# Batch 1 of a sliding-window attention and MoE kernel: q, k and attention output turned by DMA instead of on TensorE, with a new order

## The chip, the core and the metric

The kernel runs on one core of a Trainium2 chip. The metric is the device time of one execution in microseconds (us), taken as the median of several runs of the same kernel. PE is TensorE, DVE is VectorE, ACT is ScalarE, POOL is GpSimd and SP is SyncE, which in this kernel only issues DMA transfers.

## What is computed

There are 4 batches of 768 tokens with 8 heads of 64 elements. Each query sees the first 4 keys (the sinks) and its own window of 128 keys. The attention output of the 3072 tokens, 512 wide, then goes through a two-layer network with a squared ReLU.

```python
# attention, per batch and head: q, k, v are (768, 64)
scores = q @ k.T / 8
keep = (key position < 4) | (0 <= query position - key position < 128)
a = softmax(where(keep, scores, -1e9))
x = concat over heads of (a @ v)          # (3072, 512), tokens of all batches
h = x @ w_in                              # w_in is (512, 2048)
out = (maximum(h, 0) ** 2) @ w_out        # w_out is (2048, 512)
```

## The kernel before

A batch is 6 tiles of 128 tokens, and most work goes by stages s = 0, 1, 2 of 256 tokens (two tiles). Everything is computed in bf16 with fp32 accumulation in PSUM.

Scores need q and k with the head dimension on partitions, but they are loaded with tokens on partitions. So each tile of q and k has to be turned, 128x128 at a time. Batch 0's first four tiles are loaded by SP, regrouped to bf16 and turned on PE. For tiles 4 and 5 of batch 0 and all of batch 1, POOL issues loads that cast to bf16 on the way (`load_cast`, L507, into the tile `qn`). The function `transpose` (L637) then turns them on PE into PSUM (`pt`), and `unload` copies them to `qkT` on DVE or ACT. Batch 1 is turned in two groups: tokens 0 to 511 are group 0 and tokens 512 to 767 are group 1. For batches 2 and 3 (`NATURAL`), the loads are the same kind (`load_natural`, L535), but SP issues a DMA that turns one tile of q or k, 128 tokens by 512, straight into `qkT` (L591).

For each stage, `scores` (L744) writes the products to PSUM, ACT takes the exponential (L764), DVE (L776) or POOL (L355) masks it, and `values` (L812) multiplies it with v. The sinks have their own small product for the whole group (`sink_scores`, L703, with the keys that `sink_keys`, L679, copies out of `qkT` to `kblk`). `norm` (L828, L829) divides and writes `xn_sb`, again with tokens on partitions.

The network's first layer needs these rows turned as well. For batches 0 and 1, `bridge` (L861) turns the eight 128x128 blocks of a stage on PE into `px`, in two halves, and `bridge_copy` copies them to `xT`. For batches 2 and 3, `turn_x` (L843) issues two DMAs per stage on SP that write `xT`. The name `TURNED` lists stages of batch 1 that go this way; it is empty before.

`layer1` (L890) multiplies with `w_in`, for stages 0 and 1 together in columns of 512 tokens, and for stage 2 alone in columns of 256. Batch 0 does stages 0 and 1 apart. ReLU (L901 on ACT, L903 on DVE) and squaring (L912 or L910) follow. The second layer is `layer2` (L931) for the first two stages of batch 0. It is `layer2_fast` elsewhere (L1042), which makes seven products of quarter size where eight would be needed, with sums on DVE beforehand (L1000) and afterwards (L1067, L1083, L1090). Outputs are stored by SP (L954, L1115, and at the very end L1108, L1120, L1121).

The order on every engine is written by a planner (`Plan.run`) when the kernel is built. It takes the operations that are ready, places the one with the earliest planned start, and breaks ties by a key. Each operation has a planned cost; a DMA has in addition a planned time to landing, part of which is its `margin`. `PLACES` shifts and stretches the keys of whole groups of operations, and `NUDGES` shifts single ones, by their number. `LATENCY` is the planned time of a signal between engines. What comes out is a fixed sequence of instructions for each engine, each waiting only for its own inputs and buffers. While an early part runs, `warm` (L322) fills half of each planned idle stretch of PE before 34 us with products of the identity that nobody reads.

SP is one such sequence: a store that waits for its data holds back every turn behind it. DMAs of all queues share the same 16 DMA engines.

Of the kernel before, what the change touches and what calls it, by code (L numbers as in the profile page):

```python
# [16 lines left out]
LATENCY = 0.122  # L17
# [5 lines left out]
    ('att', 0, 0): (-2.46, 0.47, -0.66), ('att', 0, 1): (-0.14, 1.62, -0.14), ('att', 0, 2): (-1.375, 1.42, -0.64),  # L23
    ('att', 1, 0): (0.765, 0.89, 0), ('att', 1, 1): (-0.28, 2.29, -0.72), ('att', 1, 2): (0.08, 1.3, -0.06),
    ('att', 2, 0): (-0.07, 1.27, 0), ('att', 2, 1): (1.14, 0.56, -0.28), ('att', 2, 2): (-1.285, 1.05, -0.48),
    ('att', 3, 0): (0.09, 1.14, 0.06), ('att', 3, 1): (0.4, 1.06, -0.08), ('att', 3, 2): (-0.465, 1.16, -0.56),
    ('ev', 0, 2): (-0.46, 0.74, 0.02), ('ev', 1, 0): (-0.01, 0.91, -2.78), ('ev', 1, 1): (-0.165, 1.04, 0),
    ('ev', 1, 2): (-0.025, 0.87, 0.02), ('ev', 2, 0): (0.11, 0.96, 0), ('ev', 2, 1): (-0.045, 0.93, 0.36),
    ('ev', 2, 2): (-1.3, 0.62, 1.04), ('ev', 3, 0): (0.22, 2.01, -1.96), ('ev', 3, 1): (0, 1, -0.42),
    ('ev', 3, 2): (0.04, 1.07, -0.02), ('l1', 0, 0): (-0.28, 2.16, -0.32), ('l1', 0, 1): (-0.035, 0.33, -0.46),  # L30
    ('l1', 0, 2): (1.69, 0.27, -0.42), ('l1', 1, 0): (0.825, 0.61, -0.02), ('l1', 1, 2): (-0.155, 0.96, 0.14),
    ('l1', 2, 0): (0.035, 0.76, -0), ('l1', 2, 2): (-2.375, 1.53, -0.32), ('l1', 3, 0): (0.025, 1.07, -0.42),
    ('l2', 0, 0): (0.32, 2.21, -0.22), ('l2', 0, 1): (0.44, 1.69, 0.06), ('l2', 0, 2): (-4.315, 2.49, -0.54),
    ('l2', 1, 0): (0, 1.01, 0), ('l2', 1, 1): (2.345, 1.97, 0.22), ('l2', 1, 2): (-0.41, 0.56, 0.12),
    ('l2', 2, 0): (-0.41, 0.41, -0.6), ('l2', 2, 1): (-0.47, 0.26, 0.66), ('l2', 2, 2): (0, 1.01, 0),
    ('l2', 3, 0): (-0.09, 1.06, 0), ('l2', 3, 2): (-0.12, 0.72, 2.76), ('prep', 0, 0): (4.54, 2.5, -1),
    ('prep', 0, 1): (-1.04, 0.71, -0.64), ('prep', 1, 0): (0.935, 2.5, -0.44), ('prep', 3, 0): (-0.495, 2.45, 0.1),
    ('sink', 0, 0): (-0.755, 0.62, -0.54), ('sink', 0, 1): (0.135, 0.98, -0.04),
    ('sink', 1, 0): (-0.375, 1.71, 0.04), ('sink', 1, 1): (0.365, 0.61, 0.08), ('sink', 2, 0): (-0.01, 2.21, 0.06),
    ('sink', 3, 0): (-0.045, 0.9, 0), ('sum', 0, 2): (0, 1, -0.2), ('sum', 1, 0): (0.345, 0.25, -2.82),  # L40
    ('sum', 1, 1): (-0.27, 0.85, 0.08), ('sum', 1, 2): (-0.61, 0.73, -0.3), ('sum', 2, 0): (-0.06, 0.53, 1.32),
    ('sum', 2, 1): (-0.185, 1.13, 0.06), ('sum', 2, 2): (1.225, 2.25, -1.82), ('sum', 3, 0): (-0.005, 0.78, -0.5),
    ('sum', 3, 1): (-0.08, 0.34, 0.58), ('sum', 3, 2): (-0.185, 1.76, 0.42), ('turn', 0, 0): (4.705, 1.71, -0.76),
    ('turn', 0, 1): (0.09, 1.27, -0.04), ('turn', 0, 2): (1.185, 0.93, -0.3), ('turn', 1, 0): (0, 1.04, 0),
    ('turn', 1, 1): (0.995, 1.58, 0.4), ('turn', 1, 2): (0.65, 0.38, 0.02), ('turn', 2, 0): (0.67, 0.92, 0.14),
    ('turn', 2, 1): (-0.005, 0.93, -1.56), ('turn', 2, 2): (0.105, 1.4, 0.26), ('turn', 3, 0): (-0.1, 1.13, 0.08),
    ('turn', 3, 1): (-0.045, 0.55, -0.08), ('turn', 3, 2): (0.095, 1.46, -0.1),
    ('val', 0, 0): (-3.365, 0.71, -0.66), ('val', 0, 1): (0.145, 1.37, 0), ('val', 0, 2): (-1.82, 0.34, -3),
    ('val', 1, 0): (-0.355, 1.14, 0.04), ('val', 1, 1): (1.24, 2.09, -0.76), ('val', 1, 2): (0.18, 1.66, -2.5),
    ('val', 2, 0): (4.08, 1.76, -1.82), ('val', 2, 1): (0.05, 1.41, 0), ('val', 3, 0): (-1.585, 0.72, -0.38),  # L50
    ('val', 3, 1): (0.115, 0.58, -0.88), ('val', 3, 2): (-0.1, 1.09, -0.02), ('wt', 0): (0.275, 0.55, 0.32),
}
NUDGES = {
    4: (-0.366, 1.44), 16: (0, -0.3), 17: (0.072, -1.02), 18: (-0.061, -1.08), 19: (0.005, -0.02),
    20: (0.18, -0.98), 21: (0.025, -1.52), 24: (0, -0.44), 25: (-0.338, -1.38), 26: (0.71, 1.9),
    27: (-0.006, -0.32), 28: (0.484, 0.84), 29: (0, -0.36), 30: (-0.027, 0.14), 31: (0.007, -0.26), 32: (0, -0.48),
    33: (-0.136, -2.88), 34: (-0.096, 0.58), 35: (-0.031, 0.88), 36: (-0.018, 0), 37: (0.103, 0.12),
    39: (0.084, 0.7), 41: (-0.017, 0.88), 42: (0, -0.36), 43: (-0.11, 0.72), 44: (0, -0.12), 45: (0.297, 0.68),
    46: (-0.172, -1.86), 47: (-0.011, 0), 48: (-0.112, -0.02), 49: (-0.039, 1.08), 50: (-0.207, 0.22),
    51: (-0.044, 1.66), 52: (-0.002, -0.14), 53: (-0.017, -1.04), 54: (0, -0.2), 56: (-0.203, 0.34),  # L60
    58: (0.029, -0.48), 59: (0.008, 0), 60: (0.204, -1.22), 61: (0.19, 0.54), 62: (-0.101, -1.14), 63: (-0.022, 0),
    64: (0.192, 0.18), 65: (-0.153, 0.14), 66: (0.306, 0), 67: (0, -0.12), 69: (0.192, -2.78), 70: (-0.072, 0),
    71: (-0.012, 0), 72: (0, 0.38), 73: (-0.071, -0.04), 74: (-0.001, 0.16), 75: (-0.154, 0.08), 76: (0.133, -0.02),
    77: (0.57, 1.32), 78: (0.012, 0.46), 81: (-0.043, 0.3), 82: (0.016, -2.06), 83: (0.261, -0.22), 84: (-0.009, 0),
    86: (0.047, -0.02), 87: (0.257, -0.48), 88: (-0.361, 0.4), 89: (-0.047, 0.42), 90: (0.15, 0.34),
    91: (-0.217, 0), 92: (0, -0.06), 93: (0.05, -0), 94: (-0.016, 0), 95: (0.007, 0.02), 98: (0.071, -1.36),
    99: (-0.204, 0.84), 100: (0.062, -0.24), 101: (0, 0.08), 102: (0.126, 0.34), 103: (-0.194, -0.22),
    104: (0.051, 0), 105: (-0.214, -0.16), 108: (0.126, 0), 109: (0.206, 0), 110: (0.582, 0.28), 111: (0.032, 0.44),
    113: (-0.082, 0.1), 114: (-0.531, 0.32), 115: (0.058, -0.02), 116: (-0.003, -0.42), 118: (0.141, -1.44),
    119: (-0.307, 0.3), 120: (0.009, 0.06), 121: (0.002, 0), 122: (-0.044, 0.36), 123: (-0.017, 0.24),  # L70
    125: (-0.069, 0.34), 126: (0.099, -0.44), 127: (0, 0.14), 128: (-0.238, -0.62), 129: (-0.154, -0.08),
    130: (-0.003, 0), 131: (-0.296, 0.4), 132: (-0.082, -0.32), 133: (0.024, -0.38), 134: (0.073, 0),
    135: (0.059, 0.06), 136: (0.065, 0), 137: (0.021, 0.44), 138: (-0.166, 0.68), 139: (0.012, 0.3),
    140: (0.032, -0.28), 141: (-0.189, 0), 143: (0.103, 0), 144: (0.071, -0.44), 145: (-0.059, 0),
    146: (-0.436, 0.38), 148: (0.164, -0), 150: (0.527, -1.46), 151: (-0.19, 0.24), 153: (0.033, 0), 155: (0, 0.04),
    156: (0.089, 0), 157: (0.185, -0.32), 158: (-0.173, 0.56), 159: (-0.171, 0.18), 160: (0.252, 0.52),
    161: (-0.034, 1), 162: (-0.113, 1.42), 163: (0.013, 0.48), 165: (-0.127, 0.32), 166: (0.044, 0.4),
    167: (-0.035, 0.68), 169: (0, -0.14), 170: (-0.137, 0), 171: (-0.007, 0.26), 172: (0, 0.16),
    174: (-0.066, -0.92), 175: (0.19, 0.58), 177: (0.091, 0), 178: (0.319, -0.4), 179: (-0.18, 1.08),
    180: (-0.069, 0.02), 181: (-0.338, 0.2), 182: (-0.006, -0.02), 185: (-0.471, 1.5), 186: (-0.092, 0),  # L80
    187: (0.214, -0.08), 188: (0.107, -0.42), 189: (0.232, 0), 190: (0.088, 0), 192: (0, -0.16), 193: (-0.003, 0),
    194: (-0.01, -0.06), 196: (0.202, -0.16), 197: (0.001, -0.26), 198: (-0.511, 0), 199: (0.009, -1.34),
    200: (0.532, 0.1), 201: (-0.061, -1.16), 202: (-0.007, 0), 204: (-0.154, 0.18), 205: (0.379, 0.36),
    206: (-0.08, 0.86), 208: (0.012, -1.06), 209: (-0.163, -1.22), 210: (-0.013, 0), 211: (0.032, 0.04),
    212: (-0.121, 0), 213: (0, -0.2), 214: (0, 1.06), 215: (0, -0.06), 216: (0.121, 0.78), 217: (-0.108, 0),
    218: (0.25, 0.48), 219: (-0.155, 0), 220: (0.299, -0.24), 221: (0, -0.16), 222: (0, -0.3), 223: (-0.2, 0),
    224: (-0.065, 0), 225: (0, -0.38), 226: (0.019, -0.14), 228: (0.152, -0.9), 229: (-0.183, -0.86),
    230: (-0.164, 0), 231: (-0.021, 0.6), 232: (0.141, 0.18), 233: (-0.345, 0.26), 236: (0.132, -2.36),
    237: (0.017, -0.1), 238: (0, 0.72), 239: (-0.152, 0.14), 240: (-0.106, 0.48), 241: (-0.058, 0.3),
# [165 lines left out]
def kernel(  # L255
# [11 lines left out]
    nc = tc.nc  # L267
# [958 lines left out]
```

## Time and profile before

| | us |
|---|---|
| median of 3 runs | 216.98 |
| lowest and highest | 216.52 and 217.19 |
| the profiled execution's own time | 216.81 |
| its span, first to last instruction | 215.1 |

| engine | busy, us | share of the span |
|---|---|---|
| PE, matmul | 207.5 | 96% |
| DVE | 145.1 | 67% |
| ACT | 117.8 | 55% |
| POOL | 88.9 | 41% |

The granted TensorE clock is 1.0 throughout. The profiled execution is 0.17 us under the median, and 1.71 us of its time lie outside of the span. Matmuls are pipelined, and their shown durations overlap: the profile gives 309 ns as the mean of one L890 product, while 16 of them in a row take 1.75 us in the chain. So the pace of PE is read from the starts of successive blocks, not from the mean duration.

### The profile page before, as it was taken

What the parts mean: (1) busy time and instruction counts of PE and PEld (TensorE: products, weight loads), DVE (VectorE), ACT (ScalarE), POOL (GpSimd) and SP (SyncE); (2) the same over time, 40 slices, a digit from 0 to 9 for tenths busy, and PEclk for the clock granted to TensorE, in tenths of its full rate; (3) what the DMA queues carried; (4) which work ended last, traced back from release to release, by engine and by line L of the source; (5) the groups of instructions that cost most, each with busy time, mean ns of one, the idle gap of its engine ahead of it and who ended that gap; (6) DMA issues with size and microseconds to landing.
All of it is one profiled execution on the core that took longest, in us unless ns stands there. A gap on an engine that the chain in (4) does not pass through costs nothing.

```text
span 215.1 us, 5182 instructions
## 1 busy us (share of the span) xinstructions
PE 207.5 (96%) x2177; PEld 161.0 (75%) x2184; DVE 145.1 (67%) x276; ACT 117.8 (55%) x147; POOL 88.9 (41%) x127
## 2 busy tenths in 40 slices
PE   7999989999999999999999999999999999999992
PEld 7759977688667688554889765884988855799892
DVE  6488446687965767966788758779983543466652
ACT  3687857538954367688651627668411046657210
POOL 7999373698988963089405002227000000000000
PEclk9999999999999999999999999999999999999999
DMA  5999999999999999999959977010142220000222
GB/s 178 259 178 207 171 202 212 160 142 199 149 144 165 189 188 156 137 126 110 141 53 139 144 174 172 12 40 0 27 76 98 97 101 0 0 5 0 98 101 98
DMA packets 93351, 26.06 MB, mean 121 GB/s; under 512 B 86800, under 2 KB 91280, under 8 KB 93328
## 3 DMA queue, kind: packets, MB, share of 16 engines
q0 software_dynamic: 69248, 12.59, 77.9%
q1 hardware_dynamic: 23896, 13.07, 30.3%
q8 instruction: 17, 0.28, 0.6%
q10 hardware_dynamic: 184, 0.07, 0.1%
q14 instruction: 6, 0.05, 0.1%
HBM read 27.30 MB, written 6.29 MB: 156 GB/s over the span
## 4 chain that ended last, share of the span: by engine, by line
PE 81%; DMA 8%; DVE 4%; POOL 3%; issue 1%; ACT 1%; POOLq 0%
PE pm L890 35%; PE py L1042 28%; PE po L812 6%; PE py L931 6%; DMA qn<-in_q_dram 5%; PE ps L744 4%; DMA w_in_sb<-in_moe_w_in_dram 4%; POOL qn L507 1%; PE pt L637 1%; POOL v L516 1%; DVE qkT L331 1%; PE ya L1042 1%; POOL vs L685 1%; PE px L861 1%; DVE r L903 1%
## 5 line engine op out<-in xcount | busy, mean ns | idle before, releaser
L890 PE MATMUL pm<-xT,w_in_sb 128*128 128x256 bf16 (+1 forms) x576 | 88.3, 309 | 0.3 <-ACT r L901 0.2
L890 PEld LDWEIGHTS <-w_in_sb 128*128 128x128 bf16 x576 | 62.4, 114 | 20.9 <-issue 2.1
L901 ACT ACTIVATE r<-pm 128x1024 bf16<-128x1024 f32 x41 | 42.0, 1025 | 38.9 <-PE pm L890 37.4
L764 ACT ACTIVATE expm<-ps 128x1024 bf16<-128x1024 f32 (+1 forms) x48 | 43.5, 951 | 12.7 <-PE ps L744 12.5
L912 DVE TENSOR_TENSOR gT<-r 128x1024 bf16<-128x1024 bf16 x34 | 24.1, 712 | 21.0 <-ACT r L901 20.6
L355 POOL TENSOR_SCALAR_AFFINE_SELECT expm<-expm 128x512 bf16<-128x512 bf16 x26 | 18.2, 725 | 44.6 <-ACT expm L764 37.2
L1042 PEld LDWEIGHTS <-gT 128*128 128x128 bf16 x336 | 31.3, 98 | 3.7 <-issue 0.3
L1042 PEld LDWEIGHTS <-sg 128*128 128x128 bf16 x240 | 22.8, 98 | 3.9 <-issue 0.9
L1042 PE MATMUL py<-wt,sg 128*128 128x256 bf16 x160 | 20.8, 273 | 0.1
L1042 PE MATMUL py<-wt,gT 128*128 128x256 bf16 x160 | 20.7, 273 | 0.0
L1042 PE MATMUL py<-w_out_sb,gT 128*128 128x256 bf16 x144 | 18.7, 273 | 0.0
L812 PEld LDWEIGHTS <-expm 128*128 128x128 bf16 x352 | 16.3, 97 | 2.3 <-issue 0.9
L829 DVE TENSOR_TENSOR xn_sb<-po,rc 128x512 bf16<-128x512 f32 (+1 forms) x28 | 17.2, 615 | 1.0
L812 PE MATMUL po<-v,expm 128*128 128x65 bf16 x352 | 17.3, 193 | 0.3 <-DMA v<-in_v_dram 0.3
L776 DVE TENSOR_TENSOR expm<-expm,tri 128x1024 bf16<-128x1024 bf16 x19 | 13.4, 711 | 4.8 <-ACT expm L764 4.8
L931 PE MATMUL py<-w_out_sb,gT 128*128 128x512 bf16 x57 | 14.6, 380 | 0.5 <-issue 0.2
L910 ACT ACTIVATE gT<-r 128x1024 bf16<-128x1024 bf16 x14 | 14.7, 1058 | 0.3
L744 PE MATMUL ps<-qkT 64*128 64x128 bf16 (+1 forms) x256 | 14.6, 238 | 0.0
L744 PEld LDWEIGHTS <-qkT 64*128 64x128 bf16 x256 | 8.0, 94 | 7.4 <-issue 5.7
L329 ACT ACTIVATE osb<-py 128x256 f32<-128x256 f32 (+1 forms) x13 | 5.6, 434 | 13.2 <-PE py L1042 7.7
L812 PE MATMUL po<-vs,es 128*128 128x65 bf16 x128 | 12.7, 193 | 0.0
L545 POOL DMA_DIRECT2D v<-in_v_dram x12 | 10.6, 901 | 4.0 <-PE po L812 4.0
(79 smaller groups left out, 244.2 us busy)
## 6 DMA issues: line engine op xcount, KB each, us to landing
out_dram<-osb SPq DMA_DIRECT2D x11, 512.0 KB, 3.7
v<-in_v_dram POOLq DMA_DIRECT2D x24, 128.0 KB, 6.0
qn<-in_k_dram POOLq DMA_DIRECT2D x20, 128.0 KB, 6.8
qn<-in_q_dram POOLq DMA_DIRECT2D x20, 128.0 KB, 6.6
w_in_sb<-in_moe_w_in_dram POOLq DMA_DIRECT2D x4, 512.0 KB, 9.0
w_out_sb<-in_moe_w_out_dram POOLq DMA_DIRECT2D x4, 512.0 KB, 10.7
qr<-in_k_dram SPq DMA_DIRECT2D x4, 256.0 KB, 5.0
qr<-in_q_dram SPq DMA_DIRECT2D x4, 256.0 KB, 4.8
```

The lines of the kernel that those rows point to most:

```text
L355: nc.gpsimd.affine_select(out=e_tile, in_=e_tile, compare_op=ALU.is_ge, fill=fill, base=i - 1, pattern=[[0, n], [1 if i else -1, 128]], ch ...
L744: nc.tensor.matmul(ps[:, h2, o:o + w], lhsT=qkT_sb[r, m, 1, c, :], rhs=qkT_sb[r, m, 0, qb:qb + w // 128, :], start=(i == 0 and not biased) ...
L764: nc.scalar.activation(out=x[:, :, o:512], in_=bank_t["s", b, s, m][:, :, o:512], func=AF.Exp, scale=scale)
L776: nc.vector.tensor_mul(y, y, tri.rearrange("p (o a) c -> p o (a c)", o=1).to_broadcast([128, 4, 256]))
L812: touch(("po", b, s, m0), e, nc.tensor.matmul(pv[:, i, h2, :], lhsT=lhsT, rhs=rhs, start=(n_ == 0), stop=(n_ == len(mms) - 1)), j)
L829: touch(("po", b, s, m0), e, nc.vector.tensor_tensor(out=xn_sb[:, 2 * s:2 * s + 2, 128 * (m0 + j0):128 * (m0 + j0 + nj)].rearrange("p i (j ...
L890: nc.tensor.matmul(pm[:, i, :], lhsT=w_in_sb[:, fb // 4, kb, fb % 4:512:4], rhs=xT[:, c0 // 256:(c0 + cw) // 256, kb, :], start=(kb == 0), ...
L901: nc.scalar.activation(out=o, in_=h, func=AF.Relu)
L910: nc.scalar.activation(out=g, in_=r, func=AF.Square)
L912: nc.vector.tensor_mul(g, r, r)
L931: touch((b, u), e, nc.tensor.matmul(pm[:, i, :], lhsT=gT_sb[t // 4][:, fb, 128 * (t % 4):128 * (t % 4) + 128], rhs=w_out_sb[:, fb, :], sta ...
L1042: ins = nc.tensor.matmul(y_, lhsT=x[:, i, :], rhs=r_, start=(first or tail and n == 2) and i == 0, stop=i == HB - 1, skip_group_check=not ...
```

## The change

For batch 1, tokens 512 to 767 of q and k (tiles 4 and 5) are no longer turned by PE and unloaded by DVE or ACT. Four DMAs on SP turn them into `qkT`, one for each tile of q and of k. The attention output of stages 1 and 2 of batch 1 (tokens 256 to 767) is turned by four DMAs on SP instead of `bridge` and `bridge_copy` (`TURNED = (1, 2)`). Stage 0 of batch 1 and all of batch 0 stay on PE. For the DMA's sake, `qkT` of batch 1 is laid out as that of batches 2 and 3, tile by tile, and `unload` writes it in pieces of 128 columns. The planner's values are all new: `LATENCY`, all of `PLACES` and `NUDGES`, and a margin for the loads of `load_cast`. So the order of nearly everything differs.

```diff
-LATENCY = 0.122
+LATENCY = 0.147
...
 PLACES = {
...
-    ('l1', 0, 2): (1.69, 0.27, -0.42), ('l1', 1, 0): (0.825, 0.61, -0.02), ('l1', 1, 2): (-0.155, 0.96, 0.14),
...
+    ('l1', 0, 2): (-0.105, 1.39, 0), ('l1', 1, 0): (4.84, 1.89, 0.56), ('l1', 1, 2): (0.665, 0.41, 0.1),
...
@@ load_cast
-                dma_op("pool", ("qk", b, ti, t), run, 0.9, None, takes)
+                dma_op("pool", ("qk", b, ti, t), run, 0.9, None, takes).margin = 0.3 if b else 1.2
@@ attention
-        if b in NATURAL:
+        if b in NATURAL or b == 1:
             qkT_sb = qkT_all[b % 2].rearrange("p (t i m c) -> p m i t c", t=NT, i=2, m=NP)
@@ stage
             w = 2 if n == 2 and t0 else 1
-            for m in range(0, NP, w) if b not in NATURAL else ():
+            if b == 1 and g == 1:
+                for ti in (1, 0):
+                    for t in (4, 5):
+
+                        def turn(e, ti=ti, t=t):
+                            nc.sync.dma_start_transpose(out=qkT_sb[:, :, ti, t, :], in_=qn_t[b, ti][:, t, :])
+                        o_ = ops["turn", b, ti, t] = op(
+                            at(0.1), {"sp": 1.25}, turn, dma=0.3, reads=[qn_slot[b, ti]],
+                            after=[ops["qk", b, ti, t]])
+                        o_.margin = 5.167
+                        copies.append(o_)
+                for m in range(NP):
+                    ops["copies", b, m, g] = list(copies)
+            for m in range(0, NP, w) if b not in NATURAL and (b, g) != (1, 1) else ():
@@ unload
-                                                 t0 // 128:last // 128, :].rearrange("c i a b -> c i (a b)"),
-                                       bank_t[b, m, g][:, j, 0:512].rearrange("c (i x) -> c i x", i=w))
+                                                 t0 // 128:last // 128, :],
+                                       bank_t[b, m, g][:, j, 0:512].rearrange("c (i a b) -> c i a b", i=w, b=128))
@@
-    NATURAL, TURNED, BIASED = (2, 3), (), 1
+    NATURAL, TURNED, BIASED = (2, 3), (1, 2), 1
```

Built, the changed kernel has on PE 24 fewer products (each with its weight load): 32 turns fewer and 8 more products of `warm` (64 for 56). On SP it has 8 more turns (44 for 36). On POOL one conversion of `qs` goes elsewhere, and the masks (L355) are 18 instructions where they were 26, four masks having gone to DVE.

## The prediction

> **What bounds the kernel now.** I read the page's busy shares and chain first, then PE's timeline where it pauses, then the landing times of the DMAs on SP.
>
> ```profile
> PE 207.5 (96%) x2177; PEld 161.0 (75%) x2184; DVE 145.1 (67%) x276; ACT 117.8 (55%) x147; POOL 88.9 (41%) x127
> PE 81%; DMA 8%; DVE 4%; POOL 3%; issue 1%; ACT 1%; POOLq 0%
> ```
>
> PE carries 81% of the chain that ends last. The DMA part lies at the start and at one pause. The rows of the waits for PE say how little it stands still:
>
> ```profile
> PE pt L322 <- POOL ident L379: 1.5, 1, 1.5
> PE pt L637 <- DMA qn<-in_q_dram: 0.9, 2, 0.7
> PE po L812 <- DMA v<-in_v_dram: 0.3, 1, 0.3
> ```
>
> The columns are total, times and longest. After the start there is one pause worth a name, at 27 us:
>
> ```profile
> 27.21 0.28 PE L637 MATMUL pt<-ident,qn 128*128 128x128 bf16 x2
> 27.65 0.23 PE L637 MATMUL pt<-ident,qn 128*128 128x128 bf16 x1 [0.17 <-DMA qn<-in_q_dram]
> 28.61 0.45 PE L637 MATMUL pt<-ident,qn 128*128 128x128 bf16 x5 [0.73 <-DMA qn<-in_q_dram]
> ```
>
> By starts, two turns at 27.21 should end at 27.32, and the next begins at 27.65 (0.33 late); one more should end at 27.70, and the next begins at 28.61 (0.91 late). So 1.2 us go to the last q tiles of batch 0. From 30 to 211 us I find under 1.5 us of pauses between blocks. PE's throughput is the bound, so work taken off it counts nearly in full, and any new pause of it does too.
>
> **What the Trainium skill says.** "VectorE: DVE Perf Modes", section "The three transpose paths", gives 390 ns for a 128x128 turn on TensorE and 1309 ns by DMA. The trace differs where it matters: eight turns in a row advance the chain by 0.45 us, 56 ns each, which "TensorE: Matmul & The Clock Gate", section "Wait — 56ns, not 53.3ns?", gives as the spacing at full clock. I use the trace's 56 ns. "DMA: Bandwidth & Descriptors", section "Issuing engines are not separate DMA queues", says that transfers of all queues share 16 engines and interleave. The trace agrees: turns land 2.4 us after issue when nothing is loading, and up to 9.8 us when loads are.
>
> **What is removed.** Turns of q and k of tokens 512 to 767 are two blocks of eight (55.5 and 62.0 us in the chain or timeline). Bridges of stages 1 and 2 are two more (73.4 and 84.1 us). Here are three of the four places:
>
> ```profile
> 61.99 0.45 PE pt L637 x8
> 73.37 0.45 PE px L861 x8
> 83.90 0.83 PE L861 MATMUL px<-ident,xn_sb 128*128 128x128 bf16 x12
> ```
>
> Four blocks by 0.45 us are **1.8 us** off PE, all of it on the path. DVE and ACT lose eight copies of 512 columns (`qkT` 487 ns on DVE and 596 on ACT, `xT` 422 and 594), about 4 us. I cost this at nothing: DVE is 67% busy. Without that slack it would be a gain.
>
> **What is moved at the front.** In the new order six blocks of `layer1` (1.75 us each) stand ahead of the turns of tiles 4 and 5 of batch 0, where there were five. POOL's order of loads up to them is nearly the same. So PE reaches these turns at about 27.2 + 1.75 = 28.95 us, when the tile that landed at 28.6 is there. I take **1.2 us** as gained, with bounds 0 and 1.4 (a landing 1.2 us later takes all back). What may be late next is `w_out`: issued at 22.2 and landed 10.1 us later, at 32.3, while the new order wants it near 34.4. It is covered by 2 us. Eight more products of `warm` are 8 x 56 ns = 0.45 us if they fill nothing, none if they fill pauses; I take 0.3. Before 16 us PE waits for regrouping and exponentials in a chain that the page doesn't split; I bound the new order there at 0.5 us either way and take nothing.
>
> **What is added: eight turns on SP.** Each holds SP for 1.2 to 1.4 us, 10 us in all, in a stretch (50 to 90 us) where SP mostly waits. Their data share the DMA engines with the loads of batches 2 and 3. What matters is whether each lands before PE comes to it. The landing depends on when it is issued (median of turns by time of issue: 6.6 us at 58 to 60, 6.2 at 60 to 70, 9.3 at 70 to 85). I walk PE's new order from the first stage-2 block of `layer1` of batch 0 (43.4 us before), with these paces from the chain: a `layer1` block 1.75, an eighth of `layer2` 0.86, a product of `layer2_fast` 0.875, scores of two head pairs 0.55 (0.44 in stage 0), values 0.73 (0.36). All times below have the 1.2 us taken off.
>
> - *q and k of tiles 4 and 5.* Their loads land by about 55 us as before. SP turns them after the first store (50.4) and the first group's needs, landing by 62. Their scores come at about 67. Covered by 5 us. Scores read the new layout at the same pace: batch 1's and batch 2's both take 0.55 in the chain.
> - *Stage 1's output.* `layer1` of stages 0 and 1 comes after 30.5 us of PE work, at 43.4 + 30.5 - 1.2 = 72.7. The second of its two turns stands on SP behind three turns of batch 2 and behind the store of the second stage of batch 0, whose last product ends at 63.7. Evacuation (0.7) and the store's issue (0.4) put the turn at 64.9. It lands 5.6 to 9.3 us later, 70.5 to 74.2. Taken at 6.5, it is covered by 1.3 us; at worst it stalls PE by 1.5.
> - *Tile 3 of batch 2's q* is turned behind the store of batch 0's third stage, which ends on PE at 72.7. With 1.7 us as between product and next SP issue, it goes at 74.4 and lands at 83.7 (9.3). Its scores come at 84.7. Covered by 1.0.
> - *Stage 2's output*, turned by about 79.2, lands at 84.7 to 89.0 and is wanted at 89.4. Covered by 0.4 at least.
>
> The new order also brings the first group's sink product nearer to its keys: turns end at 51.5, four copies and `kblk` took 1.9 us before, and the product is due at about 53.3. That may cost 0.1 to 0.5.
>
> Four narrow covers will not all hold. I take **1.0 us** of new pauses, with bounds 0 and 5.
>
> **Sum.** 216.81 - 1.8 - 1.2 + 0.3 + 1.0 = 215.1 for an execution like the profiled one. The median lies 0.17 us above that execution: **215.3 us**.
>
> **Rivals.**
> - *All covers hold.* Then 1.0 and 0.3 fall away: 214.0 us. For it: PE's waits before are as good as none in the same stretch. Against it: 9 us landings. Chance 0.15.
> - *The front pause stays, and pauses of 1.5 us give back the rest.* 216.98 - 1.8 + 0.3 + 1.5 = 217.0 us. For it: four loads ahead of these tiles run into a queue with 10 us landings, and the last one may be as late again. Chance 0.13.
> - *The turn of stage 1's output is late, and the kernel slower.* SP is in order, and ahead of this turn stand batch 2's q tiles. Their loads, issued until 57, landed 4.5 us later before; with four turns more in flight they may take the 8.4 us that loads issued at 71 took, 65.4. Two turns (1.3 each) put SP at 68.0, and 9.3 us to landing make 77.3, where PE stands since 72.7: 4.6 us. That gives 216.98 - 3.0 + 0.3 + 4.6 = 218.9 us. It decides from 3.4 us of lateness, a landing after 76.1. Against it: loads issued between 53 and 65 landed in 4.2 to 6.8 us. Chance 0.24.
> - *The change doesn't take the work off PE.* The built order has 32 turns fewer, so only `warm` could stand in for them, and that is counted.
>
> **How the numbers follow.** About 0.3% (0.65 us) is what a measurement can tell from no change, so faster is under 216.33 and slower over 217.63. The forecast has 0.48, and with the rival of full cover faster has 0.62; the slightly off cases go to same, 0.14, and slower has 0.24. The likeliest case alone runs from 213.9 to 216.6. The range goes down to 213.3 (full cover, and the front better by its bound) and up to 218.0, which takes in the third case and the nearer part of the late turn.
>
> **What would show it right or wrong.** L637 and L861 should count 80 and 32 products on PE (96 and 48 before), and SP's turns 44. PE's wait for `qn` near 28 us should be gone. The row of L890's weight load near 73 us tells most: a wait on `xn_sb`'s turn there of over 3 us is the slower rival. If PE's pauses sum to as little as before and the time is not under 216, the paces that I used are wrong.

## The result, and the profile after

The changed kernel takes **224.22 us** (median of 4 runs, 223.43 to 225.71) beside 216.89 us for the kernel before. The ratio is 1.0347, 95% interval [1.0284, 1.041]. (Here and below, ratios leave out disturbed executions, so a ratio can differ from that of the medians beside it.) The forecast was 215.3 us with a range up to 218.0. So the kernel is slower where I had said faster, and by more than the rival on that side (218.9).

The profiled execution took 223.43 us. From its page come the span, the busy shares, PE's slices and granted clock in 40 slices of 5.5 us, and the chain by engine:

```profile
span 221.6 us, 5139 instructions
PE 208.5 (94%) x2155; PEld 159.5 (72%) x2160; DVE 142.4 (64%) x274; ACT 121.6 (55%) x150; POOL 81.2 (37%) x114
...
PE   7899799999999749999999999999999999999992
...
PEclk9999999999999967999999999999999999999999
...
PE 84%; DMA 9%; POOL 2%; ACT 2%; DVE 1%; issue 1%; SPq 0%; POOLq 0%
```

PE shows 22 instructions fewer (24 as built; a trace can lack a few) and is nevertheless busy 1.0 us longer. Slices 14 to 16 (72 to 89 us) show why: PE stands still in the first two of them (7, then 4 tenths), and in the last two its clock falls to 6 and 7 tenths. The waits of PE, with total, times and longest, name the pause:

```profile
PE pm L905 <- DMA xT<-xn_sb: 4.0, 1, 4.0
PE pt L324 <- POOL ident L381: 1.5, 1, 1.5
PE pm L905 <- ACT r L916: 1.1, 1, 1.1
PE pt L652 <- DVE qs L333: 0.7, 2, 0.6
```

The first row is `layer1` (now L905) of stages 0 and 1 of batch 1, waiting for the turn of stage 1's output. The row for `qn` that stood here before is gone, and a ReLU wait (L916) stands in its place. PE's timeline shows both places; the columns are start, length from first start to last end, line, operation and tiles, count, and the pause ahead:

```profile
26.08 5.40 PE L905 MATMUL pm<-xT,w_in_sb 128*128 128x256 bf16 x48 [1.11 <-ACT r L916]
...
75.77 1.05 PE L1057 MATMUL py<-w_out_sb,gT 128*128 128x256 bf16 x8
80.81 3.57 PE L905 MATMUL pm<-xT,w_in_sb 128*128 128x512 bf16 x8 [3.98 <-DMA xT<-xn_sb]
84.31 0.82 PE L759 MATMUL ps<-qkT 64*128 64x256 bf16 x8
```

Eight products of L1057 take 0.875 us by starts, so the next block could have begun at 76.65. It began at 80.81, **4.15 us** late. Those eight products of 512 columns then advance the chain by 3.57 us where the chain of before has 1.73 for eight such products:

```profile
93.39 1.73 PE pm L890 x8
```

The eight scores behind take 0.76 instead of 0.44, and the 24 products with v 1.13 instead of 0.73. That is 1.84 + 0.32 + 0.40 = **2.56 us** lost after the pause, at half the clock.

Why the turn was late stands on SP's timeline. L607 are the four new turns of q and k, L593 those of batch 2, L858 the turns of stage 1's output, L969 a store:

```profile
53.80 6.48 SPq L607 DMA_TRANSPOSE qkT<-qn  x4
63.83 1.19 SPq L593 DMA_TRANSPOSE qkT<-qn  x1
65.11 1.23 SPq L858 DMA_TRANSPOSE xT<-xn_sb  x1
66.43 5.23 SPq L593 DMA_TRANSPOSE qkT<-qn  x3
71.76 0.53 SPq L969 DMA_DIRECT2D out_dram<-osb  x1
72.34 1.30 SPq L858 DMA_TRANSPOSE xT<-xn_sb  x1
```

The second turn of stage 1's output goes out at 72.34, behind three turns of batch 2 and the store. It landed 8.33 us later by the chain:

```profile
72.34 8.33 DMA xT<-xn_sb
```

Batch 2's first turn, before which nothing can move, left SP at 63.83. SP's own waits say what it waited for:

```profile
SPq L593 <- DMA qn<-in_k_dram: 3.4, 1, 3.4
```

Its loads of q and k had landed late. The answer on `load_natural` (L537) for the loads issued between 53 and 58.7 us says:

```profile
L537 POOL DMA_DIRECT2D qn<-in_k_dram x2: 893/899/905, 55.3 to 56.2; - x2
L537 POOL DMA_DIRECT2D qn<-in_q_dram x2: 903/908/913, 57.0 to 57.9; - x2
...
DMA to landing us min/median/max: 8.4/9.5/10.2
```

In the kernel before, the same question (its line is L535) answers:

```profile
DMA to landing us min/median/max: 4.2/4.5/4.7
```

**The account.** I split the span at the first stage-2 block of `layer1` of batch 0 (43.42 us before, 44.66 after). From there to PE's last product it is 167.55 us before and 172.82 after: 5.27 us more. The parts are 1.8 less for the turns, 4.15 for the pause, 2.56 for the clock, and 0.36 that is left over, about what the small pauses differ by. The front, all that lies ahead of this block, is 1.24 us longer. The sum, 6.5 us, is the difference of the two profiled spans; the medians lie 7.3 us apart.

### The profile page after: what moved, and what is told of

It reads as the page before. It is cut to its first block, busy times and chain, and to the rows that moved or that the text cites. A ratio compares the mean times of both kernels' runs of the same rounds, so it can differ in the third digit from the quotient of the medians.

```text
span 221.6 us, 5139 instructions
## 1 busy us (share of the span) xinstructions
PE 208.5 (94%) x2155; PEld 159.5 (72%) x2160; DVE 142.4 (64%) x274; ACT 121.6 (55%) x150; POOL 81.2 (37%) x114
## 4 chain that ended last, share of the span: by engine, by line
PE 84%; DMA 9%; POOL 2%; ACT 2%; DVE 1%; issue 1%; SPq 0%; POOLq 0%
PE pm L905 39%; PE py L1057 24%; PE py L946 6%; PE po L827 6%; PE ps L759 4%; DMA xT<-xn_sb 4%; DMA v<-in_v_dram 4%; DMA vs_in<-in_v_dram 1%; POOL v L518 1%; PE pt L652 1%; ACT expm L779 1%; POOL vs L700 1%; PE ya L1057 1%; PE px L876 1%; PE pk L718 1%
## 5 line engine op out<-in xcount | busy, mean ns | idle before, releaser
L905 PE MATMUL pm<-xT,w_in_sb 128*128 128x256 bf16 (+1 forms) x576 | 89.7, 312 | 5.1 <-DMA xT<-xn_sb 4.0
L905 PEld LDWEIGHTS <-w_in_sb 128*128 128x128 bf16 x576 | 62.6, 115 | 26.7 <-issue 8.9
L916 ACT ACTIVATE r<-pm 128x1024 bf16<-128x1024 f32 x43 | 44.0, 1024 | 43.9 <-PE pm L905 42.3
L927 DVE TENSOR_TENSOR gT<-r 128x1024 bf16<-128x1024 bf16 x33 | 22.8, 690 | 23.0 <-ACT r L916 22.8
L1057 PEld LDWEIGHTS <-gT 128*128 128x128 bf16 x336 | 31.3, 98 | 4.6 <-issue 0.8
L357 POOL TENSOR_SCALAR_AFFINE_SELECT expm<-expm 128x512 bf16<-128x512 bf16 x18 | 11.6, 673 | 59.2 <-ACT expm L779 59.1
L1057 PEld LDWEIGHTS <-sg 128*128 128x128 bf16 x240 | 22.8, 98 | 3.7 <-issue 0.5
L1057 PE MATMUL py<-wt,gT 128*128 128x256 bf16 x160 | 20.7, 273 | 0.5 <-DVE osb L1082 0.3
L1057 PE MATMUL py<-wt,sg 128*128 128x256 bf16 x160 | 20.8, 273 | 0.0
L791 DVE TENSOR_TENSOR expm<-expm,tri 128x1024 bf16<-128x1024 bf16 x23 | 16.4, 715 | 3.8 <-ACT expm L779 3.5
L1057 PE MATMUL py<-w_out_sb,gT 128*128 128x256 bf16 x144 | 18.7, 273 | 0.0
L827 PE MATMUL po<-v,expm 128*128 128x65 bf16 x352 | 17.8, 194 | 0.4 <-DMA v<-in_v_dram 0.2
L843 DVE RECIPROCAL rc<-po 128x8 f32<-128x8 f32 (+1 forms) x28 | 5.5, 195 | 16.4 <-PE po L827 16.1
L925 ACT ACTIVATE gT<-r 128x1024 bf16<-128x1024 bf16 x15 | 15.7, 1056 | 0.3
L946 PE MATMUL py<-w_out_sb,gT 128*128 128x512 bf16 x59 | 15.1, 380 | 0.3
L537 POOL DMA_DIRECT2D qn<-in_q_dram x12 | 10.6, 888 | 9.5 <-DMA qn<-in_k_dram 5.5
```

The source lines that it names most:

```text
L357: nc.gpsimd.affine_select(out=e_tile, in_=e_tile, compare_op=ALU.is_ge, fill=fill, base=i - 1, pattern=[[0, n], [1 if i else -1, 128]], ch ...
L791: nc.vector.tensor_mul(y, y, tri.rearrange("p (o a) c -> p o (a c)", o=1).to_broadcast([128, 4, 256]))
L827: touch(("po", b, s, m0), e, nc.tensor.matmul(pv[:, i, h2, :], lhsT=lhsT, rhs=rhs, start=(n_ == 0), stop=(n_ == len(mms) - 1)), j)
L905: nc.tensor.matmul(pm[:, i, :], lhsT=w_in_sb[:, fb // 4, kb, fb % 4:512:4], rhs=xT[:, c0 // 256:(c0 + cw) // 256, kb, :], start=(kb == 0), ...
L916: nc.scalar.activation(out=o, in_=h, func=AF.Relu)
L925: nc.scalar.activation(out=g, in_=r, func=AF.Square)
```

## The experiments

Theory: two losses make the slowdown, a late second turn of stage 1's output (with the half clock that follows), and a slower front. Rivals: the DMAs' contention is not involved and only the order on SP is; the half clock costs nothing by itself; the front is as good as before. Most kernels here change the order alone. In them the planner runs to its end first, its planned operations are then rearranged in a list, and instructions are emitted from that list:

```diff
-            o.run(e)
+            order.append((o, e, start, start - engine.get(e, 0.0)))
...
+        for o, e, self.now, self.gap in arranged(order):
+            o.run(e)
```

`move(order, what, ahead_of)` takes one operation to a place ahead of another. "The part from 43 us on" below is the time from the first stage-2 block of `layer1` of batch 0 to PE's last product.

### 1. The second turn of stage 1 right behind the first

```diff
 def arranged(order):
+    move(order, (('turn', 1, 1), 'turn_x', (3,)), (('prep', 2, 0), 'turn', (0, 1, 1, 1)))
     return order
```

> The changed kernel with one edit: on SP the second turn of batch 1's stage-1 output stands right behind the first, ahead of three turns of batch 2 and one store. Theory 'late turn': in the changed kernel this turn went at 72.3 us, landed at 80.7, PE stood still for 4.1 us from 76.7 and ran at half clock for some 3.5 us after. Issued at about 66.4 and landing by 75, it takes both away: 224.2 - 4.1 - 3.5 = 216.6 us, up to 218.5 if batch 2's turns are next to be late; granted clock 1.0. Rival 'everything on the DMA engines is late': the pause comes back at the next use of a turned tile, 221 us or more.

Measured: 221.69 us (220.05 to 223.35), ratio 1.0224 [1.0153, 1.0295]. SP now issues both turns together (start, length, line, count):

```profile
65.69 2.63 SPq L875 DMA_TRANSPOSE xT<-xn_sb  x2
```

The waits of PE show the 4.0 gone from this place, and another in the first row:

```profile
PE pm L922 <- DMA xT<-xn_sb: 2.5, 1, 2.5
PE pt L669 <- DVE qs L350: 2.1, 1, 2.1
PE pt L341 <- POOL ident L398: 1.5, 1, 1.5
PE pm L922 <- ACT r L933: 1.1, 1, 1.1
PE py L1074 <- DVE osb L1099: 0.8, 1, 0.8
PE ps L776 <- DMA qkT<-qn: 0.6, 1, 0.6
```

The first row is now the turn of stage 2, at 98.4 us: its second turn stood until 91.25 on SP behind a turn of batch 2, 8.45 us after the first. So the place on SP made the pause near 80 us, and with that mended the next turn in the same situation is late. The time is the one that I had given for the rival (221 us or more), not for the theory; run 5 tells the two apart. The part from 43 us on took 170.3 us. The front of this execution was poor as well: PE waited 2.1 us for regrouped q or k (2.30 by starts), and its clock was 0.60 between 8 and 12 us.

### 2. The pause filled with products that nobody reads

```diff
+            if b == 1 and c0 == 0 and not late.get('filled'):
+                late['filled'] = True
+                for _ in range(64):
+                    nc.tensor.matmul(pm[:, 0, 0:128], lhsT=ident, rhs=ident, start=True, stop=True)
```

> The changed kernel with 64 products of the identity (64 x 56 ns = 3.6 us), read by nobody, on PE just before the layer1 block that waits for the late turn. Theory 'the pause costs twice': the wait stays until about 80.8 us, but PE doesn't fall to half clock, so 224.2 - 3.5 = about 220.7 us. Rival 'the slow pace after the pause has another cause' (operands that DMAs are writing around, say): still 224.2.

Measured: 222.44 us (220.34 to 222.63), ratio 1.0234 [1.0185, 1.0283]. The windows of the changed kernel (from:to, length, busy time of PE, PEld, DVE, ACT and POOL with their instructions, clock, then two values on DMA that aren't used here):

```profile
70.00:80.00 10.00, 6.39 (x82) 4.89 (x76) 6.69 (x14) 3.88 (x4) 5.67 (x8) 0.95 1.60 181
80.00:90.00 10.00, 9.20 (x59) 4.52 (x60) 3.31 (x9) 4.63 (x6) 2.63 (x4) 0.71 1.94 174
```

And those of the filled kernel:

```profile
70.00:80.00 10.00, 9.47 (x142) 8.22 (x139) 6.50 (x15) 3.88 (x4) 5.30 (x7) 1.00 1.54 175
80.00:90.00 10.00, 8.27 (x74) 4.77 (x72) 3.66 (x9) 5.33 (x6) 2.42 (x4) 1.00 1.75 171
```

The clock goes from 0.71 to 1.00. The block that waits begins at 82.39, 1.6 us later than in the changed kernel, since the turn landed later still; so the time is 1.7 us over the 220.7 expected. From there the last product is 134.4 us away, against 136.7 in the changed kernel. So the slow clock is a loss of its own, 2.3 us by this comparison and 2.56 by the pace of the blocks. Filling it takes the clock's share away and leaves the wait.

### 3. q and k of tiles 4 and 5 not turned at all

```diff
-    nc.sync.dma_start_transpose(out=qkT_sb[:, :, ti, t, :], in_=qn_t[b, ti][:, t, :])
+    nc.vector.memset(qkT_sb[:, :, ti, t, :], 0.0)
```

> The changed kernel without its four DMA turns of q and k of tokens 512 to 767: DVE writes zeros there in their place, so batch 1's last 256 tokens get wrong scores. All else stands in the same order. Theory 'the added turns push the loads back': the loads of batch 2 issued at 55 to 58 us land in about 5 us instead of 8.4 to 10.2, SP reaches the second turn of stage 1 at about 68.5, it lands by 76, the pause is nearly gone: about 216.5 to 218 us. Rival 'only the order on SP is at fault': the loads land as late as with the turns, the pause stays over 3 us, 223 us or more.

Measured: 221.02 us (218.96 to 221.66), ratio 1.0174 [1.012, 1.0228], between the two times expected. Batch 2's loads, issued between 55.0 and 57.7, now landed after 5.3/5.5/6.1 us instead of 8.4/9.5/10.2. The four turns had thus cost them 4 us, and SP came to stage 1's second turn at 69.45, 2.9 us sooner. It is no earlier because SP is busy without a stop from batch 2's first turn on, with five turns and the store:

```profile
61.30 1.30 SPq L593 DMA_TRANSPOSE qkT<-qn  x1
...
69.45 1.31 SPq L858 DMA_TRANSPOSE xT<-xn_sb  x1
```

The pause shrank but did not go:

```profile
74.78 1.05 PE L1057 MATMUL py<-w_out_sb,gT 128*128 128x256 bf16 x8
78.44 3.35 PE L905 MATMUL pm<-xT,w_in_sb 128*128 128x512 bf16 x8 [2.61 <-DVE expm L791]
```

It is 2.78 us by starts, and PE began 9.0 us after the turn's issue. The profile names a mask on DVE, which had ended at 77.83, 0.6 us earlier; the turn is the likelier releaser, but that isn't shown. The half clock came here too (3.28 us for the eight products by starts). It is not in every execution of this kernel: the three with a mean granted clock of 0.992 took 220.66 to 221.66 us, the one with 1.000 took 218.96. So contention explains a part of the lateness. The place on SP weighs more: run 1 leaves the contention as it is, moves the turn, and this pause is gone.

### 4. The front of the kernel before

```diff
+    order = front + order[179:]
```

`front` holds the first 179 planned operations in the order, on the engines and with the PSUM pools of the kernel before.

> The changed kernel with the first 179 operations (all up to the first layer1 block of batch 0's stage 2) in the order, on the engines and in the PSUM pools that the kernel before has. PE reached that block at 43.4 us before and at 44.8 in the changed kernel. Theory 'the front's loss is hidden by the late turn': PE comes 1.4 us earlier to the wait, which still ends near 80.7, so 223.5 to 224.2 us. Rival 'the loss is carried through': 222.8 us.

Measured: 221.75 us (218.36 to 222.33), ratio 1.014 [1.0052, 1.0227]. The wait for ReLU at 26 us is gone from PE's rows, and the pause of the second turn is there (3.55 us by starts). But this execution's stage-2 block began at 44.56, hardly earlier than in the changed kernel (44.66): PE waited 1.1 us for q or k that DVE regroups and 1.1 us for `qn`. The ratio rests on two executions that lie 3.1 us apart (218.36 and 221.50), and the time fits neither of the two expected. By itself this run doesn't settle what the front costs; runs 5 and 9 do it better.

### 5. Both pairs of turns together on SP

```diff
 def arranged(order):
     move(order, (('turn', 1, 1), 'turn_x', (3,)), (('prep', 2, 0), 'turn', (0, 1, 1, 1)))
+    move(order, (('turn', 1, 2), 'turn_x', (5,)), (('prep', 2, 0), 'turn', (2, 1, 0, 4)))
     return order
```

> As 'second turn ahead', and in addition the second turn of stage 2's output stands on SP right behind its first, ahead of a turn of batch 2 that waited for its load. That one-move kernel had its next pause, 2.7 us at 98 us, on this turn. Theory 'each pause is one late turn on SP': that pause goes too, 221.7 - 2.5 = about 219 us. Rival 'everything on the DMA engines is late': the wait moves on to scores of batch 2 or the next turn, 221 us or more.

Measured: 219.11 us (217.21 to 222.64, 11 runs), ratio 1.0091 [1.006, 1.0122]. SP's timeline has both pairs:

```profile
67.20 2.65 SPq L876 DMA_TRANSPOSE xT<-xn_sb  x2
...
83.75 2.59 SPq L876 DMA_TRANSPOSE xT<-xn_sb  x2
```

No wait for `xT` is left among PE's larger rows. The part from 43 us on takes 46.42 to 213.97, that is 167.55 us, that of the kernel before. Two moved DMAs give back all 5.27 us. That the two lengths are equal to the last digit is chance: run 5 has 1.8 us less of turns, and pauses of about 2.6 us by starts where the kernel before has 1.1. What is left in this execution lies in the front: PE waited twice for v (0.8 us each) near 17 us, and the clock was 0.77 to 0.81 from 16 to 24 us.

### 6. Batch 2's v loaded after its q and k

As run 5, with one edit more:

```diff
...
+    sorted_ = [x for x in loads if x[0].name[0] == 'qk'] + [x for x in loads if x[0].name[0] == 'v']
...
```

> As 'both turns ahead', and on POOL the six loads of batch 2's v come behind its twelve loads of q and k instead of between them. The turns of batch 2's q and k then find their data up to 4 us earlier. If what is left is that SP waits for these loads: 1 to 2 us under 'both turns ahead', about 217.5. If what is left is the landing time of the turns on loaded DMA engines: the same as 'both turns ahead'.

Measured: 219.95 us (218.59 to 223.37), ratio 1.0107 [1.0052, 1.0162]; the part from 43 us on is 168.4 us. Here PE waits 0.8 us for `xT` and 0.9 for `qkT`; neither stands among the rows of run 5. The order of these loads was not what was left.

### 7. The kernel before with four turns that nobody needs

```diff
+    def extra():
+        for ti in (1, 0):
+            for t in (4, 5):
+                nc.sync.dma_start_transpose(out=xT_sb[1][:, ti, :, 128 * (t - 4):128 * (t - 4) + 128], in_=qn_t[1, ti][:, t, :])
```

They are emitted on SP ahead of batch 2's first turn, where the changed kernel has its own four.

> The kernel before, with four more DMA turns on SP ahead of batch 2's first turn (the tiles 4 and 5 of batch 1's q and k, into a part of xT that is overwritten later; nobody reads them). PE's work and order are those of before. Theory 'the added turns push the loads back': batch 2's loads issued at 55 to 58 us land in 8 to 10 us instead of 4.2 to 4.7, and the time rises little (217 to 218.5 us), since before's order asks later for what comes by SP. Rival 'the loads were late because of the changed order': landings as before, 216.9 us.

Measured: 217.41 us (216.87 to 218.55, 20 runs), ratio 1.002 [1.0008, 1.0032]. The same loads as above:

```profile
L553 POOL DMA_DIRECT2D qn<-in_k_dram x2: 893/899/905, 53.5 to 54.4; - x2
L553 POOL DMA_DIRECT2D qn<-in_q_dram x2: 903/908/913, 55.3 to 56.2; - x2
...
DMA to landing us min/median/max: 7.4/8.3/8.9
```

8.3 us instead of 4.5: four turns hold these four loads up by 3.8 us, near 1 us each, in a kernel where nothing else is changed. The loads issued between 67.5 and 71 us landed after 15.2 us (median) instead of 7.7, but by then batch 2's own turns had moved as well. Yet the part from 43 us on is 167.55 us once more. Contention is real, and it costs this kernel only about 0.4 us: no row of PE's waits in it names a turn.

### 8. The kernel before once more

No edit; one profiled execution, to see how its parts vary.

> The kernel before, the same instructions in the same order, profiled once more. If its front is steady, the first layer1 block of stage 2 of batch 0 starts within 0.3 us of the 43.4 us of the first profile; if the first loads land differently from run to run, it comes up to 1.2 us later, as in the runs of the changed kernel and of its graft with before's front (44.4 to 45.5).

Measured: 217.34 us. The stage-2 block begins at 43.92, 0.5 us later than in the first profile, and the part behind is 167.55 us again. So the front varies from execution to execution, and in three profiles of this order (before, 7 and 8) the rest doesn't.

### 9. The front of before, and both pairs together

```diff
...
+    order = front + order[179:]
+    move(order, (('turn', 1, 1), 'turn_x', (3,)), (('prep', 2, 0), 'turn', (0, 1, 1, 1)))
+    move(order, (('turn', 1, 2), 'turn_x', (5,)), (('prep', 2, 0), 'turn', (2, 1, 0, 4)))
```

> The changed kernel with both remedies: the first 179 operations as in the kernel before, and on SP the second turns of batch 1's stages 1 and 2 right behind their first ones. From batch 0's first stage-2 block of layer1 on, 'both turns ahead' took as long as the kernel before (167.5 us to the last product in both), and what it lost lay in the front (46.4 us for 43.4 to 43.9). Theory 'two separate losses, front and late turns': 216.9 to 217.5 us, no different from before. Rival 'the front was slow by chance of that run and not by its order': 218.5 us or more, as with 'both turns ahead'.

Measured: 217.06 us (215.03 to 221.18, 22 runs) beside 217.24, ratio 0.9994 [0.9975, 1.0013]. Undoing these two things undoes the slowdown. The changed kernel with both is level with the kernel before and not 1.8 us faster. PE's waits show where that gain went:

```profile
PE ps L974 <- DMA qkT<-qn: 1.0, 2, 0.6
...
PE pm L1120 <- DMA xT<-xn_sb: 0.6, 1, 0.6
```

By starts the pauses of the part from 43 us on are 0.52 and 0.82 for `qkT` at 76.6 and 99.7, 0.73 for `xT` at 124.7, and three of about 0.3 elsewhere: 3.1 us. The kernel before has 1.1 us of its own there. The 2.0 us between them take up the 1.8 us saved, and the part measures 167.9 us.

### 10. Batch 2's first scores one block later

As run 9, with one edit more:

```diff
+    second = [x for x in order if tag(x[0]) == (('l1', 1, 0), 'mm', ())][1]
+    for what in ((('att', 2, 0), 'expo', (0, 1, 128)), (('att', 2, 0), '<lambda>', ((0, 1),))):
+        x = order.pop(next(i for i, y in enumerate(order) if tag(y[0]) == what))
+        order.insert(order.index(second) + 1, x)
```

> As 'front and turns', and the scores of batch 2's first two head pairs in stage 0 (with the first of their exponentials) stand one layer1 block of 1.73 us later on PE. They were waited for in 'both turns ahead' (1.2 us at 81 us) and 'v loads behind' (1.1 us at 80 us). Theory 'they come before their turned tiles': 0.5 to 1.2 us under 'front and turns', 216.0 to 216.6, which would be faster than before. Rival 'the wait is one for ACT or a PSUM bank and moves along': the same as 'front and turns'.

Measured: 217.38 us (217.04 to 218.14, 14 runs), ratio 1.0012 [0.9995, 1.0028]. The 0.52 us wait for `qkT` is gone, and one for ReLU stands there, 1.08 us by starts at 83.65:

```profile
PE pm L1124 <- ACT r L1135: 0.9, 1, 0.9
```

In this one profile the wait has moved along and not gone; whether the later scores cause the wait for ReLU isn't shown. No version here beats the kernel before.

## Why the prediction was wrong

- **The 1.8 us off PE** are there: L652 and L876 count 80 and 32 products, and SP has 44 turns. Run 5 and run 9 show that the order behind gives them back in small waits, even without the large one.
- **"Evacuation (0.7) and the store's issue (0.4) put the turn at 64.9."** This step failed. The second turn of stage 1's output went at 72.34, 7.4 us later than in my walk. The step names batch 2's turns as standing ahead but lets only the store hold the turn back. Two things were wrong in it, and run 3 tells them apart. I took the landings of batch 2's loads from the trace of before, where four turns less were in flight; with them the loads took 9.5 us instead of 4.5 (runs 3 and 7), and the first turn of batch 2 left SP only at 63.83. That is 2.9 us of the 7.4. The other 4.5 remain in run 3, where the loads land after 5.5 us: I had no term for the time that SP itself spends on the turns ahead, 8.2 us in run 3 and 8.5 in the changed kernel from batch 2's first turn to this one. The loads of batch 1's tiles 4 and 5, which I had landing by about 55, landed from 53.8 to 57.1; nothing on PE waited for their turns.
- **"Taken at 6.5".** The landing took 8.33 us, inside of my bounds of 5.6 to 9.3, at their far side. PE came to the block at 76.65 instead of 72.7: 2.5 us of that is the front, 1.5 the walk from there. Had PE been on time and the turn not, the pause would have been 8 us.
- **"1.0 us of new pauses, with bounds 0 and 5."** The pause of 4.15 us alone stays within these bounds, at their far side. The clock was in no term, put at nothing without a reason. The Trainium skill, "TensorE: Matmul & The Clock Gate", section "What's actually happening", has TensorE fall to half clock after an idle window of about 3.4 us. The pause of 4.15 us agrees with that. But the clock also halved behind shorter pauses: 2.78 us (run 3), 2.30 (the front of run 1), and two of about 1 us each, one close behind the other (run 5, near 17 us). It did not halve behind 2.69 us (run 1, at 98 us), nor behind two of about 1 us at the same place in run 2. So the length of one pause doesn't decide it here. I had a rival with a pause of 4.6 us and didn't add what the half clock then costs, 2.56 us in this trace.
- **"I take 1.2 us as gained" at the front.** The wait for `qn` near 28 us did go. But in its place PE waits 1.28 us by starts at 26.1 us for a ReLU: on ACT it ran from 25.01 to 26.03, directly after the products that it reads, so PE stood waiting for a buffer. I looked for the next late thing among the loads (`w_out`), not among the PSUM buffers that six blocks of `layer1` in a row need; that these buffers are the reason is my reading of the trace, not an experiment. The rival "the front pause stays" was right on this point. That wait is in every run with the new front (the changed kernel, 1, 2, 3, 5 and 6) and in none with that of before.
- **The rival of the late turn** named the right turn, the right queue and the right cause, and its sign, a wait of over 3 us there, came. It has SP at 68.0 (72.34) and a pause of 4.6 us (4.15). Its sum came out 5.3 us under the result, mostly for two reasons: the clock (2.5), and the front, counted there as a gain of 1.2 where the account has a loss of 1.24. What I held against it, loads that landed in 4.2 to 6.8 us, was evidence from a kernel without the added traffic.
- **The three other narrow covers** (tile 3 of batch 2's q, stage 2's output, the sink product): stage 2's output is late as soon as stage 1's isn't (run 1). In the changed kernel the first pause hides that. Scores of batch 2 wait 0.7 us for `qkT` in run 1 and 0.5 and 0.8 in run 9; for which tile isn't shown. The sink product of the first group doesn't wait in the changed kernel and waits 0.3 us in runs 4, 9 and 10.

**Open.** The stage-2 block of batch 0 begins between 44.4 and 46.4 us with the new front and between 42.9 and 44.6 with that of before. The 1.28 us are in every profile with the new front; the rest comes with waits for v and for regrouped q and k, in runs 1 and 5 with half clock behind them, and no run here takes it apart. The releaser of the pause in run 3 is not settled, nor what makes a single turn's landing as long as 8 to 9 us, nor when a pause halves the clock.

## What to carry to other kernels

Work moved from an engine to DMA was paid for here in the landing times of other transfers in flight, so a landing read from the trace before holds only for the traffic of before (4.5 us became 9.5). On a queue that runs in order, look at what stands ahead of each transfer that PE needs, and at what that in turn waits for: here two moved instructions were worth 5.27 us. Where PE is the bound, price a pause of 2 us or more, or several short ones close together, at its length plus a possible stretch at half clock behind it. If it can't be avoided, filling it with products that nobody reads saves the second part (2.3 us in run 2).

## What the runs showed of the hardware

- A pause of 4.15 us on PE cost 6.7 us: 2.56 us came after it, when PE worked at half clock for 5 us. The clock also fell to half behind pauses of 3.55 and 2.78 us (runs 4 and 3), and with 64 filling products it stayed at 1.00 (run 2). A shorter pause isn't safe: 2.30 us (run 1) and two of about 1 us (run 5) halved it too, while 2.69 us (run 1) and two of about 1 us (run 2) didn't.
- A turn of 128x512 bf16 by DMA, 131 KB, held other loads up by close to 1 us (3.8 us for four, run 7; about 4 us less without the four, run 3). The Trainium skill, "Advanced Engine Details and Errata", section "X-Bar Transpose (TRN2)", has turns "as fast as regular DMAs" at 350 to 400 GB/s, which would be an estimate of 0.33 to 0.37 us each. The hold-up in run 7 is nearly three times that.
